# Five written orders of TensorE's four-slot blocks are replaced, and one gate comes due two slots earlier

## The chip, the cores and the metric

The kernel runs on one core of a Trainium2 chip. The time is the device time of one execution in microseconds (us). TensorE (PE) multiplies matrices into the eight banks of PSUM; ScalarE (ACT), VectorE (DVE) and GpSimd (POOL) work on the results; SyncE (SP) issues all transfers. TensorE's 128 rows are used in two ways here: as one array of 128 rows, or as two halves of 64 rows, rows 0 to 63 (half 0) and rows 64 to 127 (half 1), each with matmuls of its own.

## The reference

```python
xn = _layernorm(x, axis=-1)                       # x: 1 x 2048 x 512
qkv = (xn @ wqkv)                                 # 32 heads of 16
scores = einsum("bhqd,bhkd->bhqk", q, k) * 16**-0.5
o = einsum("bhqk,bhkd->bhqd", softmax(scores), v)
s = o.reshape(B, S, D) @ wo
h = relu(xn @ w1 + b1) ** 2                       # 512 -> 1792
g = silu(h @ w2 + b2)                             # 1792 -> 512
out = x + s * g
```

Attention with 32 heads over 2048 tokens and a dense block with a squared ReLU both start from the normalized x; their product is added to x.

## The kernel before

**Staging.** A lead-in normalizes x, makes q, k and v and parks them in DRAM. Then a loop of 512 slots does attention. A slot is one unit `u` (four heads and 512 queries; 32 units) and one block `kb` of 128 keys (16 per unit). For each slot TensorE computes four score tiles of 128 keys by 512 queries (`exp_mm`, line 1245), one per head; ACT takes exp of each into a tile `pt` in SBUF (line 1251); and two slots later four matmuls of 128 rows, one per head, add V times these to the unit's bank `po` (`pv_mm`, line 389, called by `pv_step`). In the trace each of the four appears twice, so that a po group of eight belongs to one slot, and one of sixteen to two.

**Row maxima.** The shift of the softmax needs each query's maximum over all keys before its unit starts. For a later unit, `max_mm` (line 308) computes scores with queries as rows, 128 by 512, and DVE reduces each tile to its row maxima (line 316). Fourteen or sixteen such tiles are made in four slots while they last.

**Dense work.** Between them run the matmuls of the dense block and, near the end, of the output projection (line 244 and line 806), which `dense()` yields as blocks of work for four slots. A dense matrix product is cut by rows: half 0 does its share of the sum first, half 1 adds its share to the same bank afterwards. The first product (`first_pair`) uses matmuls of 256 columns, two to a unit of work; the second (`second`) and the output projection use one of 512 columns. Dense work has one bank, `pd_t` (bufs=1): the copy out of it on ACT (line 598 or 784) must end before the next tile may start. For the same reason the first matmul that half 1 does in a bank waits (`add_manual_dep`) for a consumer of a later matmul of half 0.

**Banks of the scores.** Two rings of three banks, `se` and `pm_t`. An exp's scores go to `se` and a maximum's to `pm_t`, unless the order says otherwise. Each ring is used in turn: a matmul that takes a bank waits until the reader of the matmul three places back in that ring is done.

**The written orders.** `long_slots` issues TensorE's work of four slots from strings. Two characters are one step: a letter and the row half. `D` is a unit of dense work, `s` the scores of an exp in an `se` bank and `S` in a `pm_t` bank, `m` a maximum in a `pm_t` bank and `M` in an `se` bank. The order of TensorE is manual, so a string is the order in its queue; ACT's exps, DVE's reductions and the copies follow in the same order on their own engines, which are manual too in the loop (`LOOP`). An order is a tuple of strings, the texts; after each text comes the po group of the one or two slots that it covers (`sizes`). `pick` chooses the order of a block:

- `TWO_TWO` (two texts), `ONE_TWO_ONE` and `TWO_ONE_ONE` (three) for dense blocks while 16 or 17 exp tiles are to be had;
- `FIRST_FEW` and `SECOND_FEW` (sizes 2, 1, 1) where there are fewer than 17, which is 14: `FIRST_FEW` in the blocks at slots 4, 8 and 12, before the tiles `mt` are added at slot 16, and `SECOND_FEW` at slots 444 and 448, after the tiles `ex` have been given up;
- `MIXED` (four texts of one slot) for the block in which two tiles of the second dense product meet: six matmuls of each half end tile 0, and six of each half begin tile 1. It comes once in each of the eight chunks, at slots 44, 100, 156, 212, 268, 324, 380 and 436;
- `WO_INNER` (sizes 1, 2, 1) at slots 452, 456, 460, 468, 472 and 476 and `WO_END` (2, 1, 1) at slot 464, for the output projection of the last tokens, in which half 0 has twelve dense matmuls and half 1 has nine. From slot 480 on other orders are used again.

**The gate.** After a tile of the second dense product, `tile_post` (line 596) copies it out on ACT (`u`, line 598) and adds b2 on POOL (line 599). `gate` (line 574) then does a tanh on ACT (line 578), two steps on POOL (lines 579 and 580) and, four slots on, a store to `g_d`. `later(n, fn)` runs a step at the beginning of the n-th slot after the current one, when `begin` calls `run_waiting`, that is ahead of that slot's own work on every engine. In the chunks before the last one the gate goes through `behind` to the next po group; in the last chunk it is issued when it is due.

Of the kernel before, what the change touches and what calls it, by code (L numbers as in the profile page):

```python
# [28 lines left out]
NCK = S // CW  # L29
# [19 lines left out]
    "M0S1S0S1M1M0",  # L49
)  # L50
FIRST_FEW = (
    "D0D0S1D0M1D0S1M1D0S1D0D0m1s1D0m1D0M1D0M1S1D0D0M0S1",
    "M0s1D1D1s0m0S0D1m0D1D1D1s0D1M0D1s0S0D1D1S0D1m0D1M0",
    "s0s1m0m1S0M1",
)
SECOND_FEW = (
    "D0s1m1D0D0D0D0s1D0M1S1D0S1D0M1s1D0D0m1m1D0D0M1m1s0",
    "S1M0M0D1D1S0S0D1D1M0D1D1s0D1m0S0D1D1D1D1s0S0M0D1M0",
    "m1s0M0m0S1s1",
)  # L60
MIXED = (
    "m1s1D0m1D0m1D0s1D0M1D0D0S0s1",
    "D1D1M0S0D1D1D1s0m0S0M0D1M1S0",
    "m1D0s1D0s1D0D0m1D0s1D0S1m0M1",
    "D1D1D1M0S0D1M0D1S0S0D1M0M0S1",
)
WO_INNER = (
    "s0m1D0D0M1D0D0S1D0D0m1D0s1D0S1D0D0M1D0S1s1S1m0D0M1S0M1",
    "S0D1m0D1s0D1m0s0D1D1D1D1S0M0D1D1m0s0M1m0",
    "m0s1s0S1m1M0",  # L70
)
WO_END = (
    "M1S0M0S1D0D0m1D0D0s1S1D0D0D0D0D0M1S1D0M1s1S1D0D0m1m1M0",
    "M1S0s0m0D1D1D1m0D1s0D1m0D1s0D1s0D1m0s0D1",
    "S1M0s1m1s0m0",
)
LEAD_AT = (
    (3, 8, 12, 17, 22, 26, 31, 36, 40, 45, 48),
# [5 lines left out]
def kernel(  # L84
# [54 lines left out]
    with ExitStack() as ph:  # L139
# [87 lines left out]
        def later(n, fn, first=False):  # L227
            waiting.insert(0 if first else len(waiting), (now[0] + n, fn))
# [7 lines left out]
        def block(parts, kind, between={}):  # L236

            units, ends, posts = [[], []], [[], []], []
            for mms, per, first, post in parts:

                def emit(ms, lane, follow):
                    r = slice(64 * lane, 64 * lane + 64)
                    for out_, lh, rh, first_, last_ in ms:
                        mm = nc.tensor.matmul(  # L244
                            out_(), lh(r), rh(r),
                            start=first_ and lane == 0, stop=last_ and lane == 1,
                            skip_group_check=True,
                        )
                        if follow is not None:
                            tc.add_manual_dep(  # L250
                                mm.ins, follow.ins.name,
                                mybir.DependencyInfo(
                                    mybir.DependencyClass.Sync, mybir.DependencyReason.DATA
                                ),
                                reason="the other row tile is done with the bank",
                            )
                            follow = None

                for lane in range(2):
                    free = first and lane == 0  # L260
                    for k in range(0, len(mms), per):
                        units[lane].append(
                            lambda m=mms[k : k + per], lane=lane, k=k, free=free, emit=emit: [
                                emit(m, lane, None if k or free else last_use[0]),
                                lane and k // per in between and between[k // per](),
                            ]
                        )
                    ends[lane].append(len(units[lane]))
                posts.append(post)
            return units, ends, posts, kind  # L270

        def terms3(ps, terms):

            n = len(terms)
            out_ = []
            for t, (lh, rh) in enumerate(terms):
                for i, (a, b) in enumerate(((0, 0), (0, 1), (1, 0))):
                    out_.append((
                        ps if callable(ps) else lambda: ps,
                        lambda r, lh=lh, a=a: lh(a, r),  # L280
                        lambda r, rh=rh, b=b: rh(b, r),
                        t == 0 and i == 0, t == n - 1 and i == 2,
                    ))
            return out_
# [165 lines left out]
        def mlp_tasks(mp):  # L450
# [120 lines left out]
            def second(c):  # L571
                hT = state["hT"]

                def gate(u, tt):
                    th = rs[tt].rearrange("p a b -> p (a b)")

                    def gate_ops():
                        nc.scalar.activation(th, u, AF.Tanh, scale=0.5)
                        nc.gpsimd.tensor_scalar(th, th, 0.5, 0.5, op0=ALU.mult, op1=ALU.add)
                        nc.gpsimd.tensor_tensor(u, u, th, op=ALU.mult)  # L580
                        t0 = c * CW + tt * P
                        later(4, lambda: nc.sync.dma_start(g_d[t0 : t0 + P, :], u))

                    if c < NCK - 1:
                        behind.append(gate_ops)
                    else:
                        gate_ops()

                sums = {}

                def tile_sum(tt):
                    if tt not in sums:
                        sums[tt] = pd.tile([P, D], F32, name="pd_t")
                    return sums[tt]

                def tile_post(tt):
                    u = up.tile([P, D], F32, name="u")
                    nc.scalar.activation(u, sums[tt], AF.Copy)  # L598
                    nc.gpsimd.tensor_tensor(u, u, b2_t, op=ALU.add)  # L599
                    later(3, lambda: gate(u, tt))  # L600

                mms = []
                for tt in range(2):
                    ts_ = slice(tt * P, (tt + 1) * P)
                    mms.append(terms3(lambda tt=tt: tile_sum(tt), [
                        (
                            lambda a, q, fo=fo, ts_=ts_: hT[q, a, fo, ts_],
                            lambda b, q, fo=fo: w2t[q, b, fo],
                        )
                        for fo in range(FO)  # L610
                    ]))
                for k in range(0, 36, 12):
                    yield block([(mms[0][k : k + 12], 1, k == 0, None)], "second")
                yield block(
                    [
                        (mms[0][36:], 1, False, lambda: tile_post(0)),
                        (mms[1][:6], 1, True, None),
                    ], "mixed",
                )
                for k in range(6, 42, 12):  # L620
                    if c == NCK - 1 and k == 18:
                        gone_pt.extend(rot["ex"])
                        free_pt[:] = [t for t in free_pt if all(t is not x for x in gone_pt)]
                        tiles[0] -= 3
                    yield block(
                        [(mms[1][k : k + 12], 1, False, None if k < 30 else lambda: tile_post(1))],
                        "second",
                    )
# [532 lines left out]
        for i in range(NT + 3):  # L1161
# [32 lines left out]
            if i >= 5:  # L1194
                rest.append(("v", (i - 3) % 4, (i - 3) // 4))
                if i % 4 == 2:
                    c = (i - 3) // 4
# [409 lines left out]
```

## Time and profile before

| | us |
|---|---|
| time, median of 3 runs | 1610.49 |
| lowest and highest | 1609.7, 1610.57 |
| the profiled execution | 1609.88 |
| its span, first to last instruction | 1608.1 |
| PE busy in it | 1592.1 |
| DVE busy | 1341.7 |
| ACT busy | 1185.4 |
| granted TensorE clock | 0.999 |

The profile shows one execution. In its timeline a row has start, duration, engine, line, operation, the names of output and inputs, the number of instructions merged, and in brackets the idle time before it and what ended that. A tile's name tells the kind of matmul: `se` and `pm_t` at line 1245 are scores for an exp, at line 308 scores for a maximum, `pd_t` is dense work, `po` the product with V. The row half is not shown; it follows from the string. The ends of matmuls are modelled, their starts are recorded.

### The profile page before, as it was taken

The page shows a single profiled execution, that of the slowest core. Times are in us where ns is not written, and L with a number is a line of the kernel's source. Part 1 is how long each engine was busy: PE and PEld are TensorE (multiplying, and loading weights), DVE is VectorE, ACT ScalarE, POOL GpSimd, SP SyncE. Part 2 cuts the span into 40 slices and gives each one's busy share as a digit, 9 for nine tenths or more (in the row PEclk, how much of TensorE's full clock was granted, in tenths as well). Part 3 has the DMA queues.
Part 4 walks back from the last instruction along what each step waited for, and adds up shares of the span by engine and source line. Part 5 has one row for each costly group of instructions (what it writes and reads, how often), then busy time and mean ns, then how long its engine had stood idle before and what let it go on. Part 6 is the DMA issues. An engine that isn't in the chain of part 4 may idle for free.

```text
span 1608.1 us, 35737 instructions
## 1 busy us (share of the span) xinstructions
PE 1592.1 (99%) x13639; PEld 992.3 (62%) x13639; DVE 1341.7 (83%) x2327; ACT 1185.4 (74%) x2345; POOL 525.4 (33%) x549
## 2 busy tenths in 40 slices
PE   8999999999999999999999999999999999999998
PEld 6888666566556655665566556655665565555555
DVE  6499888988888888888888898889888998888833
ACT  6311687778778877887788778877877787777785
POOL 6645687132213310331133112302321223213334
PEclk9999999999999999999999999999999999999999
DMA  8795664334233532442243514342432432325353
GB/s 302 237 275 193 215 197 140 108 107 128 58 87 103 153 92 63 122 127 67 80 127 104 123 44 145 102 108 57 138 99 77 106 123 57 103 76 147 112 170 138
DMA packets 150467, 201.45 MB, mean 125 GB/s; under 512 B 50008, under 2 KB 67416, under 8 KB 148760
## 3 DMA queue, kind: packets, MB, share of 16 engines
q1 hardware_dynamic: 150296, 199.17, 42.2%
q8 instruction: 107, 1.75, 0.5%
q14 instruction: 64, 0.52, 0.1%
HBM read 144.84 MB, written 53.99 MB: 124 GB/s over the span
## 4 chain that ended last, share of the span: by engine, by line
PE 98%; DVE 1%; ACT 0%; issue 0%; DMA 0%; POOL 0%; DVEq 0%; SPq 0%; ACTq 0%
PE po L389 30%; PE pd_t L244 23%; PE pm_t L308 12%; PE se L1245 10%; PE se L308 6%; PE pm_t L1245 4%; PE se L1006 3%; PE se L1047 3%; PE pd_t L806 2%; PE po L1047 2%; PE pd_t L1047 1%; DVE mx L316 1%; PE pm_t L1106 1%; ACT pt L1251 0%; PE pm_t L842 0%
## 5 line engine op out<-in xcount | busy, mean ns | idle before, releaser
L316 DVE TENSOR_REDUCE mx<-pm_t 128x1 f32<-128x512 f32 x1374 | 878.6, 682 | 133.0 <-PE pm_t L308 78.8
L1251 ACT ACTIVATE pt<-se 128x512 f32<-128x512 f32 x1073 | 599.2, 620 | 82.4 <-PE pm_t L308 41.1
L308 PE MATMUL pm_t<-ka,qm 64*128 64x512 f32 x1374 | 541.2, 412 | 1.9 <-ACT pt L1251 0.7
L389 PE MATMUL po<-pt,v 128*32 128x512 f32 x3456 | 511.5, 601 | 0.0
L1245 PE MATMUL se<-qe,ka 64*128 64x512 f32 x1292 | 501.4, 421 | 0.2
L316 DVE TENSOR_REDUCE mx<-se 128x1 f32<-128x512 f32 x674 | 440.7, 682 | 57.7 <-PE se L308 29.3
L1251 ACT ACTIVATE pt<-pm_t 128x512 f32<-128x512 f32 x655 | 382.7, 609 | 136.3 <-PE pm_t L1245 86.6
L244 PEld LDWEIGHTS pd_t<-xc,w1s 64*128 64x128 f32 x2688 | 335.9, 187 | 23.0 <-ACT pt L1251 13.4
L244 PE MATMUL pd_t<-xc,w1s 64*128 64x256 f32 x2688 | 343.1, 281 | 0.0
L244 PE MATMUL pd_t<-w2t,hT 64*128 64x512 f32 x1344 | 340.9, 397 | 0.0
L308 PEld LDWEIGHTS pm_t<-ka,qm 64*128 64x128 f32 x1374 | 250.3, 184 | 96.1 <-DVE mx L316 42.0
L1245 PE MATMUL pm_t<-qe,ka 64*128 64x512 f32 x756 | 301.2, 431 | 0.0
L244 PEld LDWEIGHTS pd_t<-w2t,hT 64*128 64x128 f32 x1344 | 239.5, 184 | 78.1 <-ACT pt L1251 23.5
L1245 PEld LDWEIGHTS se<-qe,ka 64*128 64x128 f32 x1292 | 220.7, 184 | 84.0 <-ACT pt L1251 42.9
L308 PE MATMUL se<-ka,qm 64*128 64x512 f32 x674 | 254.2, 415 | 0.9
L389 PE MATMUL po<-ex,v 128*32 128x512 f32 x544 | 224.5, 601 | 0.0
L389 PEld LDWEIGHTS po<-pt,v 128*32 128x32 f32 x3456 | 95.4, 108 | 162.0 <-issue 155.8
L542 POOL TENSOR_TENSOR r<-r 128x512 f32<-128x512 f32 x56 | 58.2, 1040 | 326.2 <-ACT r L539 326.2
L308 PEld LDWEIGHTS se<-ka,qm 64*128 64x128 f32 x674 | 116.5, 184 | 76.2 <-ACT pt L1251 47.5
L1245 PEld LDWEIGHTS pm_t<-qe,ka 64*128 64x128 f32 x756 | 131.5, 184 | 18.1 <-DVE mx L316 8.4
L599 POOL TENSOR_TENSOR u<-u,b_t 128x512 f32<-128x512 f32 x16 | 20.6, 1286 | 326.4 <-ACT u L598 326.4
L1251 ACT ACTIVATE ex<-se 128x512 f32<-128x512 f32 x187 | 114.2, 624 | 10.9 <-PE pm_t L308 8.2
(139 smaller groups left out, 1410.6 us busy)
## 6 DMA issues: line engine op xcount, KB each, us to landing
w1s<-w_d SPq DMA_DIRECT2D x196, 256.0 KB
xn_d<-xT SPq DMA_DIRECT2D x8, 1024.0 KB
qm<-q_d SPq DMA_DIRECT2D x128, 64.0 KB
qe<-q_d SPq DMA_DIRECT2D x128, 64.0 KB
ka<-k_d SPq DMA_DIRECT2D x32, 256.0 KB
hl<-r_d SPq DMA_DIRECT2D x31, 256.0 KB
k_d<-hl SPq DMA_DIRECT2D x30, 256.0 KB
q_d<-hl SPq DMA_DIRECT2D x15, 512.0 KB
```

Source lines behind the costliest of these rows:

```text
L244: mm = nc.tensor.matmul(out_(), lh(r), rh(r), start=first_ and lane == 0, stop=last_ and lane == 1, skip_group_check=True,)
L308: nc.tensor.matmul(ps, qms[u][p][64 * j : 64 * j + 64, qb * P : (qb + 1) * P], kas[qd, p][64 * j : 64 * j + 64, kc * 512 : (kc + 1) * 512] ...
L316: return nc.vector.tensor_reduce(mxs[u][:, c, kc : kc + 1], ps, axis=AX.X, op=ALU.max)
L389: nc.tensor.matmul(po[32 * j : 32 * j + 32, :], vs[qd][:, (4 * kb + j) * VW : (4 * kb + j) * VW + 32], pts[j], start=(kb == 0), stop=(kb = ...
L542: nc.gpsimd.tensor_tensor(r, r, r, op=ALU.mult)
L599: nc.gpsimd.tensor_tensor(u, u, b2_t, op=ALU.add)
L806: inst = nc.tensor.matmul(ps[lane], oc[r, a, n, ts_], wot[r, b, n], start=m == 0 and (lane == 0 or wide), stop=m == kos and (lane == 1 or ...
L1006: nc.tensor.matmul(out_(), lh(slice(0, P)), rh(slice(0, P)), start=first_, stop=last_)
L1047: inst = nc.tensor.matmul(out_(), lh(r), rh(r), start=first_ and lane == lane0, stop=last_ and lane != lane0, skip_group_check=True,)
L1106: nc.tensor.transpose(pt[:, ko, :], xn[:, ko * P : (ko + 1) * P], ident)
L1245: nc.tensor.matmul(se, kas[qd, j // 2][b : b + 64, kb * P : (kb + 1) * P], qes[u][j // 2][b : b + 64, :], start=True, stop=True,)
L1251: return nc.scalar.activation(pts[j], se, AF.Exp, scale=0.25)
```

## The change

Five of the eight orders are written anew: `FIRST_FEW`, `SECOND_FEW`, `MIXED`, `WO_INNER` and `WO_END`. The number of each kind of work in a block is the same; the sequence, and with it for some matmuls the ring (small or capital letter) and the half that does a score in a given text, are others. `SECOND_FEW` has two of half 1's dense units in its third text now, which were in the second. The sizes, and `pick`, are as they were. The gate of the second tile of the last chunk becomes due one slot after its `tile_post` instead of three. As that `tile_post` now runs at slot 451 instead of 450, the gate is issued at slot 452 instead of 453.

```diff
 FIRST_FEW = (
-    "D0D0S1D0M1D0S1M1D0S1D0D0m1s1D0m1D0M1D0M1S1D0D0M0S1",
-    "M0s1D1D1s0m0S0D1m0D1D1D1s0D1M0D1s0S0D1D1S0D1m0D1M0",
-    "s0s1m0m1S0M1",
+    "D0S1M1D0D0S1m1D0D0s1D0M1S1D0D0D0M1S1D0M1S1D0D0M1m0",
+    "m0s1D1s0m0D1D1S0D1D1M0D1s0D1S0D1M0D1S0D1S0D1M0D1M0",
+    "m1s0M1S0M0S1",
 )
 SECOND_FEW = (
-    "D0s1m1D0D0D0D0s1D0M1S1D0S1D0M1s1D0D0m1m1D0D0M1m1s0",
-    "S1M0M0D1D1S0S0D1D1M0D1D1s0D1m0S0D1D1D1D1s0S0M0D1M0",
-    "m1s0M0m0S1s1",
+    "S1D0m1D0s1D0M1D0s1D0D0D0m1S1D0D0M1D0D0S1s1D0M1m1m0",
+    "m0s1D1s0D1D1m0s0D1D1m0D1s0m0D1D1D1s0s0S0D1m0M1",
+    "D1s0D1M0S1S0M0m1",
 )
 MIXED = (
-    "m1s1D0m1D0m1D0s1D0M1D0D0S0s1",
-    "D1D1M0S0D1D1D1s0m0S0M0D1M1S0",
-    "m1D0s1D0s1D0D0m1D0s1D0S1m0M1",
-    "D1D1D1M0S0D1M0D1S0S0D1M0M0S1",
+    "M1D0S1D0s1m1s1D0D0S1D0D0m0M1",
+    "m0D1D1s0D1D1m0s0D1m0D1s0s1m0",
+    "D0M1D0S1D0M1s1m1D0D0S1D0m1s0",
+    "M0D1s0m0D1S0D1s0D1S0D1D1M1M0",
 )
 WO_INNER = (
-    "s0m1D0D0M1D0D0S1D0D0m1D0s1D0S1D0D0M1D0S1s1S1m0D0M1S0M1",
-    "S0D1m0D1s0D1m0s0D1D1D1D1S0M0D1D1m0s0M1m0",
-    "m0s1s0S1m1M0",
+    "M0S1D0D0S1D0M1s1S1D0D0m1D0D0s1D0m1D0D0D0s1m1D0M1S0s1m0",
+    "s0D1M0S0D1D1m0S0M0D1D1D1s0D1m0D1D1s0m0m1",
+    "S0M1M1S1m0s0",
 )
 WO_END = (
-    "M1S0M0S1D0D0m1D0D0s1S1D0D0D0D0D0M1S1D0M1s1S1D0D0m1m1M0",
-    "M1S0s0m0D1D1D1m0D1s0D1m0D1s0D1s0D1m0s0D1",
-    "S1M0s1m1s0m0",
+    "S1M0D0S1M0D0D0M1S1D0D0s1D0m1D0S1D0s1D0D0D0m1M1D0M1m1S0",
+    "D1s0D1m0D1S0D1m0D1s0D1D1s0M0D1S0S0D1m0M1",
+    "m0s1m0S0s1M1",
 )
...
-                    later(3, lambda: gate(u, tt))
+                    later(1 if c == NCK - 1 and tt else 3, lambda: gate(u, tt))
```

## The prediction

> **What bounds the kernel now.** I read the page first, then a table of windows, then the timelines of single engines.
>
> ```profile
> span 1608.1 us, 35737 instructions
> ...
> PE 1592.1 (99%) x13639; PEld 992.3 (62%) x13639; DVE 1341.7 (83%) x2327; ACT 1185.4 (74%) x2345; POOL 525.4 (33%) x549
> ```
>
> TensorE (PE) is never free for long, so the end is the sum of its stretches, and 99% does not say whether a stretch is full: a matmul that waits for its row half still counts. I therefore cut the loop into its blocks of four slots, from one group of po matmuls (line 389) to another. Columns: window, its length, then busy time by engine.
>
> ```profile
> 290.78:302.90 12.12, 12.03 (x90) 6.11 (x89) 10.98 (x21) 9.39 (x19) 1.30 (x1) 1.00 0.04 16
> ...
> 1362.67:1373.82 11.15, 11.15 (x90) 6.18 (x88) 9.93 (x17) 8.26 (x17) 3.71 (x4) 1.00 0.52 126
> ...
> 1384.98:1397.07 12.09, 11.98 (x91) 6.05 (x89) 10.59 (x18) 9.35 (x19) 3.15 (x3) 1.00 0.66 192
> 1408.18:1419.73 11.55, 11.46 (x91) 5.93 (x89) 10.11 (x17) 8.48 (x17) 0.00 (x0) 1.00 0.37 90
> ...
> 1431.28:1442.90 11.62, 11.49 (x87) 6.10 (x85) 10.32 (x18) 9.34 (x19) 2.93 (x4) 1.00 0.16 48
> ...
> 1466.26:1477.80 11.54, 11.46 (x87) 6.08 (x86) 9.89 (x17) 9.38 (x19) 2.71 (x4) 1.00 0.51 146
> ...
> 1501.07:1512.75 11.68, 11.49 (x88) 6.13 (x86) 10.24 (x17) 8.89 (x18) 2.56 (x3) 1.00 0.56 154
> ```
>
> From the top: the first of eight MIXED blocks (slot 44); a block with the untouched ONE_TWO_ONE (slot 428); the last MIXED (slot 436; mean of the eight 12.15); the first of two SECOND_FEW (slot 444); the first of six WO_INNER (slot 452); WO_END (slot 464); the last WO_INNER (slot 476; mean of the six 11.66). With three FIRST_FEW blocks (slots 4, 8, 12) twenty blocks change. In none of these rows are ACT or DVE busy for the whole window, so neither sets its length alone.
>
> Next, the PE of slot 456, WO_INNER, whose first text begins s0 m1 D0 D0 M1 D0 D0 S1 D0 D0 m1 (letter: kind of matmul, digit: row half).
>
> ```profile
> 1442.90 1.07 PE L389 MATMUL po<-pt,v 128*32 128x512 f32 x8
> 1443.90 0.50 PE L1245 MATMUL se<-qe,ka 64*128 64x512 f32 x1
> ...
> 1444.24 0.39 PE L308 MATMUL se<-ka,qm 64*128 64x512 f32 x1
> 1444.24 0.40 PE L806 MATMUL pd_t<-wot,oc 64*128 64x512 f32 x1
> 1444.47 0.38 PE L1245 MATMUL pm_t<-qe,ka 64*128 64x512 f32 x1
> 1444.47 0.62 PE L806 MATMUL pd_t<-wot,oc 64*128 64x512 f32 x2
> ...
> 1444.93 0.39 PE L806 MATMUL pd_t<-wot,oc 64*128 64x512 f32 x1
> ...
> 1446.52 0.39 PE L806 MATMUL pd_t<-wot,oc 64*128 64x512 f32 x1
> ...
> 1447.27 0.49 PE L308 MATMUL pm_t<-ka,qm 64*128 64x512 f32 x1 [0.18 <-ACT pt L1251]
> ...
> 1447.84 0.42 PE L1245 MATMUL pm_t<-qe,ka 64*128 64x512 f32 x1
> ...
> 1448.19 1.07 PE L389 MATMUL po<-pt,v 128*32 128x512 f32 x8
> ...
> 1451.83 1.92 PE L389 MATMUL po<-pt,v 128*32 128x512 f32 x16
> 1453.68 0.49 PE L308 MATMUL pm_t<-ka,qm 64*128 64x512 f32 x1
> ...
> 1454.25 0.39 PE L308 MATMUL se<-ka,qm 64*128 64x512 f32 x1
> ...
> 1454.57 1.06 PE L389 MATMUL po<-pt,v 128*32 128x512 f32 x8
> ```
>
> **Turns.** Each half takes a matmul of 512 columns every 0.23 us (1444.24, 1444.47), the first after a po group 0.34 (1443.90 to 1444.24). M1, fifth in the text, starts with the first D0, and S1, eighth, with the second: the halves do not start in text order; one runs ahead by up to three entries of the other. So a text of n turns (its longer half) should run 0.34+0.23(n-2) from first start to last.
>
> **Floors.** A po group of eight adds 1.20: 1.00 from its start to the next text (1442.90, 1443.90), 0.32 from the last start to it (1454.25, 1454.57), 0.11 for the long first turn, less one turn. One of sixteen (1451.83, 1453.68) adds 1.85+0.32+0.11-0.23 = 2.05. Slot 428 has 29 turns and groups of 8, 16, 8 in 11.15. So WO (28 turns, same groups) could take 10.92; SECOND_FEW (29) 11.15; MIXED (28 turns, four groups of eight, 2x1.20-2.05 = 0.35 more) 11.27. Above these floors lie 8x0.88 = 7.0 in MIXED, 6x0.74 = 4.4 in WO_INNER (mean 11.66), 0.6 in WO_END, 0.8 in SECOND_FEW: 12.8 us is all that this change can reach.
>
> **What holds the halves up.** Same text of slot 456, on ACT:
>
> ```profile
> 1445.45 0.60 ACT L1251 ACTIVATE pt<-pm_t 128x512 f32<-128x512 f32 x1 [0.42 <-PE pd_t L806]
> ...
> 1446.63 1.08 ACT L1251 ACTIVATE pt<-pm_t 128x512 f32<-128x512 f32 x2
> ```
>
> The bank of S1 was written from 1444.47 to 1444.85, yet its exp starts at 1445.45, after ACT idled 0.42 for a D matmul. In the text four D0 stand ahead of this S1; the fourth runs from 1444.93 to 1445.32. A matmul is reported done only when all before it in the program are: running ahead physically does not free its bank. The second S1 (exp at 1446.63, over at 1447.23) holds the bank that m0 needs, three pm_t tiles later; m0 starts at 1447.27 instead of 1446.75, right after the D0 of 1446.52. The text's last start (1447.84) is 3.94 after its first instead of 0.34+13x0.23 = 3.33.
>
> ```profile
> PEld pd_t L244 <- ACT pt L1251: 36.9, 44, 0.8
> ```
>
> A D needs no bank from an exp, still 44 of them waited for one, 36.9 us in all: a waiting matmul also holds what stands behind it, whichever half.
>
> **MIXED**, slot 436, fourth text (D1D1D1M0S0...), PE and DVE:
>
> ```profile
> 1394.87 0.49 PE L308 MATMUL se<-ka,qm 64*128 64x512 f32 x1
> ...
> 1395.43 0.39 PE L244 MATMUL pd_t<-w2t,hT 64*128 64x512 f32 x1
> ...
> 1396.13 1.00 PE L308 MATMUL se<-ka,qm 64*128 64x512 f32 x2
> ...
> 1395.89 1.89 DVE L316 TENSOR_REDUCE mx<-se 128x1 f32<-128x512 f32 x3 [0.63 <-PE se L308]
> ```
>
> M0 is over at 1395.36, but three D1 stand ahead of it, the third until 1395.82; DVE starts at 1395.89. The fourth M0, on the first one's bank, starts at 1396.64 (1396.13 and 1.00 less its 0.49) instead of 1396.36: 0.28 lost. In a run DVE takes one every 0.60 ((1.89-0.69)/2, its last 0.69 long), ACT one every 0.48 (1.08-0.60 at 1446.63).
>
> Third text (m1D0s1D0...):
>
> ```profile
> 1388.87 0.50 PE L308 MATMUL se<-ka,qm 64*128 64x512 f32 x1
> ...
> 1391.39 0.60 ACT L598 ACTIVATE u<-pd_t 128x512 f32<-128x512 f32 x1
> ...
> 1391.81 0.49 PE L308 MATMUL pm_t<-ka,qm 64*128 64x512 f32 x1
> 1392.05 0.49 PE L244 MATMUL pd_t<-w2t,hT 64*128 64x512 f32 x1
> ```
>
> The first D0 opens the pd_t bank that copy u must empty: 0.24 late.
>
> **The change part by part.** No matmul, exp or reduce is added or removed, only their order and, for some, the bank. I walked each new text with these steps: turns of 0.23, done in program order, ACT every 0.48, DVE every 0.60, a bank free 0.05 to 0.1 after its reader ends (1447.23 to 1447.27 above).
>
> *MIXED.* Text four, M0D1s0m0D1S0..., releases M0 at 0.4; its bank is asked for at 1.26 to 1.49, and DVE is through at 1.2: 0.28 gone. Text two now has two exps ahead of copy u in ACT's queue instead of three, and they are released at 0.7 and 1.2; u starts at about 1.8 into the text instead of 2.5 (1391.39 less 1388.87), and is over before text three begins at 2.9 (1391.81): 0.24 gone. Late next are s1, m1, s1 in text one, which stand ahead of a D0 due at 0.57. They need banks that the text before has filled last:
>
> ```profile
> 1386.80 0.60 ACT L1251 ACTIVATE pt<-se 128x512 f32<-128x512 f32 x1 [0.51 <-PE pd_t L244]
> ```
>
> ACT is through with that text half a microsecond ahead of the first exp of text one, so I leave text one as it is. 8x(0.28+0.24) = 4.2.
>
> *WO_INNER.* First text M0S1D0D0S1D0M1s1S1D0D0m1...: by the walk every bank is free within 0.05 of its turn (closest: s1 after D0D0D0, m1 after S1), so 3.33 instead of 3.94 in slot 456, and about 0.58 a block. The other texts keep what they have. Five blocks: 2.9.
>
> *Gate and slot 452.* SECOND_FEW now ends its D1 in the third text, and the gate is due at slot 452 instead of 453.
>
> ```profile
> 1430.28 0.61 ACT L598 ACTIVATE u<-pd_t 128x512 f32<-128x512 f32 x1
> ...
> 1430.97 1.28 POOL L599 TENSOR_TENSOR u<-u,b_t 128x512 f32<-128x512 f32 x1 [27.04 <-ACT u L598]
> ...
> 1437.33 0.68 ACT L578 ACTIVATE r<-u 128x512 f32<-128x512 f32 x1
> ```
>
> Now the tanh comes 5 us after POOL's sum and waits for nothing. Moved, it stands ahead of all exps of slot 452. Copy u starts about 1.0 into the third text, POOL ends 0.69+1.28 later at 3.0, the text of slot 452 begins at 2.1: ACT stands until 3.0, spends 0.68, and its first exp starts 1 us late. Behind it wait that bank's m1 and the D0 after it; the text runs to 4.1, 0.8 above 3.33, the block to 10.92+0.8+0.1 = 11.8 where it took 11.62. So slot 452 loses 0.2 rather than gaining 0.58. Bounds: from that gain (sum ready earlier) to a loss of 0.8; I take -0.2, since the durations are rows. The gate's two POOL steps and its g_d store move by the same slots; POOL had idled for 27 us, and SP gets no issue that it did not have.
>
> *WO_END*: the walk finds no bank late in text one and two late by 0.05 in text two: 0.4 of the 0.62 above its floor. *SECOND_FEW*: of the 0.40 above its floor text one gives nearly all back, but text two, now one turn shorter, ends on a bank 0.1 late and on weights that come no earlier: 0.2 each, 0.4. *FIRST_FEW*:
>
> ```profile
> 181.28 0.18 PEld L244 LDWEIGHTS pd_t<-xc,w1s 64*128 64x128 f32 x1 [0.24 <-DMA xc<-xn_d]
> ```
>
> In slot 4 a D waits for xc to land, which no order changes; in slots 8 and 12 the half that holds the D runs without a gap. Nothing; between a loss and a gain of 0.3.
>
> Sum: 4.2+2.9-0.2+0.4+0.4 = 7.7. Span 1608.1 to 1600.4; the profiled run 1609.88 to 1602.2; the median of the runs, 1610.49, is 0.6 above the profiled one: **1602.8**.
>
> A rule against it: the Trainium skill, "TensorE: Matmul & The Clock Gate", Part 3, says that matmuls are monotone in start and end by program order, with only weight loads pulled ahead. The trace agrees for the end (1445.45) and not for the start (1444.24). What it would give is the first rival.
>
> **Rivals.** *Starts in text order.* Then only pairs side by side in the text share a turn. Counted so, FIRST_FEW goes from 31 to 30 turns, SECOND_FEW 33 to 31, MIXED 33 to 33, WO_INNER 31 to 32, WO_END 32 to 31: -3-4+0+6-1 = -2 turns, -0.5 us: 1610.0, and the change does not do what it says. The page named above is this rule. Against it: the two rows at 1444.24.
>
> *All floors reached*: -12.8, 1597.7. For it: weights also come early once nothing stalls. Against: three exps in a row, ACT at 0.48.
>
> *A held half holds both*, on the slower side: in MIXED's text one, s1 m1 s1 stand ahead of D0. If ACT were four exps and a copy behind there, the last bank would come free at 4x0.48+0.61 = 2.5, D0 2 us late, 8x2 = 16 against 7.7: 1618.8. It decides from 1.4 us a block ((7.7+3.3)/8). Against: the 0.51 that ACT idles at 1386.80.
>
> **How the numbers follow.** The walk 0.77, its own range 1598 to 1607 (half to all of its terms, and the gate's bounds); text-order starts 0.11; floors 0.07; held half 0.05. The range 1597 to 1607 takes in the floors and leaves out text-order starts and the held half. 0.2% is 3.2 us, about what a measurement of this kernel can tell from no change. Faster by more: 0.81 (the walk less 0.03, and the floors); within: 0.14; slower: 0.05.
>
> **What would show it.** MIXED windows near 11.6, WO_INNER near 11.1, slot 452 near 11.8 with the tanh ahead of the exps; no ACT idle of 0.4 behind a D. Wrong if D's start late behind waiting s or m in the new texts, or if the starts follow the text.

## The result and the profile after

The changed kernel takes 1602.22 us (median of four runs, 1601.52 to 1602.5), the kernel before, run beside it, 1610.29 (1609.7 to 1610.57): a ratio of 0.995, 95% interval 0.9932 to 0.9967. The profiled execution took 1601.52 us with a span of 1599.7, 8.4 less than the 1608.1 before. The forecast was 1602.8.

The page, and the same blocks as before in the table of windows (columns: window, its length, busy time by engine), from the top FIRST_FEW (slot 4), MIXED (slot 44), the untouched ONE_TWO_ONE (slot 428), MIXED (436), SECOND_FEW (444), WO_INNER (452), WO_END (464) and WO_INNER (476):

```profile
span 1599.7 us, 35747 instructions
...
PE 1585.6 (99%) x13639; PEld 991.5 (62%) x13639; DVE 1343.2 (84%) x2327; ACT 1183.2 (74%) x2345; POOL 525.2 (33%) x549
```

```profile
178.54:190.73 12.19, 12.04 (x115) 7.49 (x113) 9.96 (x17) 8.64 (x18) 8.38 (x13) 1.00 0.94 319
290.79:302.38 11.59, 11.59 (x90) 5.74 (x89) 10.96 (x21) 9.16 (x19) 1.29 (x1) 1.00 0.09 33
1358.70:1369.85 11.15, 11.15 (x90) 6.18 (x88) 9.93 (x17) 8.26 (x17) 3.50 (x4) 1.00 0.56 134
1381.03:1392.60 11.57, 11.57 (x90) 6.11 (x89) 10.69 (x18) 9.17 (x19) 3.15 (x3) 1.00 0.68 193
1403.74:1415.07 11.33, 11.33 (x90) 6.42 (x88) 9.99 (x17) 8.54 (x18) 0.00 (x0) 1.00 0.36 92
1426.47:1438.29 11.82, 11.48 (x88) 5.85 (x86) 10.25 (x18) 9.42 (x20) 5.23 (x5) 1.00 0.47 147
1460.30:1471.43 11.13, 11.13 (x87) 6.37 (x85) 10.05 (x17) 9.22 (x19) 2.69 (x4) 1.00 0.46 130
1493.44:1504.44 11.00, 11.00 (x87) 5.92 (x86) 10.00 (x17) 8.79 (x18) 2.58 (x3) 1.00 0.55 147
```

PE's share of the span says 99% in both profiles: the page cannot show this gain, the windows can. Cut at the po groups, all 127 blocks of the loop compare like this:

| blocks | before, sum | after, sum | difference |
|---|---|---|---|
| 8 MIXED | 97.17 | 92.73 | -4.44 |
| 6 WO_INNER | 69.94 | 66.84 | -3.10 |
| of these slot 452 | 11.63 | 11.82 | +0.19 |
| 1 WO_END | 11.54 | 11.14 | -0.40 |
| 2 SECOND_FEW | 23.09 | 22.72 | -0.37 |
| 3 FIRST_FEW | 34.81 | 34.85 | +0.04 |
| 107 others | | | +0.03 |

The gain stands where it was made, and the blocks between neither add to it nor give it back. Now the first text of slot 456 on PE (rows: start, duration, engine, line, tiles, count, idle time before and what ended it), with M0 S1 D0 D0 S1 D0 M1 at its head:

```profile
1439.28 0.49 PE L308 MATMUL se<-ka,qm 64*128 64x512 f32 x1
...
1439.62 0.39 PE L806 MATMUL pd_t<-wot,oc 64*128 64x512 f32 x1
1439.62 0.39 PE L1245 MATMUL pm_t<-qe,ka 64*128 64x512 f32 x1
1439.85 0.39 PE L806 MATMUL pd_t<-wot,oc 64*128 64x512 f32 x1
1439.85 0.39 PE L308 MATMUL se<-ka,qm 64*128 64x512 f32 x1
...
1442.61 0.39 PE L308 MATMUL pm_t<-ka,qm 64*128 64x512 f32 x1
1442.94 0.64 PE L389 MATMUL po<-pt,v 128*32 128x512 f32 x4
```

and on ACT:

```profile
1439.85 1.09 ACT L1251 ACTIVATE pt<-pm_t 128x512 f32<-128x512 f32 x2 [0.29 <-PE pm_t L1245]
1440.82 0.60 ACT L1251 ACTIVATE pt<-se 128x512 f32<-128x512 f32 x1
1441.30 0.62 ACT L1251 ACTIVATE pt<-pm_t 128x512 f32<-128x512 f32 x1
```

Fifteen turns take 3.33 from first to last start, where they took 3.94, and ACT no longer idles behind a D: the exp of the S1 that starts at 1439.62 follows at 0.48 from the one before it.

MIXED, slot 436. In the second and third text copy u is early, and D0 opens the third text without a wait (PE's first pair, at 1387.85):

```profile
1386.81 0.59 ACT L598 ACTIVATE u<-pd_t 128x512 f32<-128x512 f32 x1
...
1387.85 0.50 PE L244 MATMUL pd_t<-w2t,hT 64*128 64x512 f32 x1
1387.85 0.50 PE L308 MATMUL se<-ka,qm 64*128 64x512 f32 x1
```

In the fourth, DVE takes the first M0 0.54 after its start, where it took 1.02 (1395.89 less 1394.87 before), so that the last M0 starts 1.54 after the first one and not 1.77:

```profile
1390.72 0.50 PE L308 MATMUL se<-ka,qm 64*128 64x512 f32 x1
...
1391.26 0.69 DVE L316 TENSOR_REDUCE mx<-se 128x1 f32<-128x512 f32 x1 [0.38 <-PE se L308]
```

And slot 452, with the tanh ahead of its exps:

```profile
1427.07 1.28 POOL L599 TENSOR_TENSOR u<-u,b_t 128x512 f32<-128x512 f32 x1 [27.55 <-ACT u L598]
...
1428.38 0.63 ACT L578 ACTIVATE r<-u 128x512 f32<-128x512 f32 x1 [0.41 <-POOL u L599]
...
1428.72 0.39 PE L806 MATMUL pd_t<-wot,oc 64*128 64x512 f32 x1
...
1428.92 1.07 ACT L1251 ACTIVATE pt<-pm_t 128x512 f32<-128x512 f32 x2
...
1429.55 0.49 PE L308 MATMUL pm_t<-ka,qm 64*128 64x512 f32 x1 [0.34 <-ACT pt L1251]
1429.55 0.49 PE L806 MATMUL pd_t<-wot,oc 64*128 64x512 f32 x1
```

The tanh waits for POOL's sum, the first exp of the slot starts 1.46 after the text (1427.46), and m1, on the bank of that exp's scores, waits until 1429.55. The D0 behind it needs nothing of that exp. It was due one turn after the D0 of 1428.72, at 1428.95, yet it starts with m1: a matmul that waits for its bank holds the other half too.

### The profile page after: what moved, and what is told of

Read it like the earlier page. It is cut to its first block, busy times and chain, and to the rows that moved or that the text cites. A ratio compares the mean times of both kernels' runs of the same rounds, so it can differ in the third digit from the quotient of the medians.

```text
span 1599.7 us, 35747 instructions
## 1 busy us (share of the span) xinstructions
PE 1585.6 (99%) x13639; PEld 991.5 (62%) x13639; DVE 1343.2 (84%) x2327; ACT 1183.2 (74%) x2345; POOL 525.2 (33%) x549
## 4 chain that ended last, share of the span: by engine, by line
PE 98%; DMA 1%; SPq 0%; ACT 0%; DVE 0%; issue 0%; POOL 0%; DVEq 0%; ACTq 0%
PE po L389 30%; PE pd_t L244 22%; PE pm_t L308 12%; PE se L1245 11%; PE se L308 6%; PE pm_t L1245 5%; PE se L1006 3%; PE se L1047 3%; PE pd_t L806 2%; PE po L1047 1%; PE pd_t L1047 1%; PE pm_t L1106 0%; DMA xc<-xn_d 0%; DMA xt<-in_A_x_dram 0%; PE pm_t L842 0%; PE se L890 0%
## 5 line engine op out<-in xcount | busy, mean ns | idle before, releaser
L316 DVE TENSOR_REDUCE mx<-pm_t 128x1 f32<-128x512 f32 x1389 | 889.3, 684 | 129.0 <-PE pm_t L308 75.3
L1251 ACT ACTIVATE pt<-se 128x512 f32<-128x512 f32 x1101 | 616.8, 620 | 86.7 <-PE pm_t L308 47.2
L308 PE MATMUL pm_t<-ka,qm 64*128 64x512 f32 x1389 | 547.5, 411 | 1.2 <-DVE mx L316 0.6
L1245 PE MATMUL se<-qe,ka 64*128 64x512 f32 x1312 | 511.4, 420 | 0.0
L316 DVE TENSOR_REDUCE mx<-se 128x1 f32<-128x512 f32 x659 | 432.3, 683 | 52.1 <-PE se L308 33.9
L1251 ACT ACTIVATE pt<-pm_t 128x512 f32<-128x512 f32 x626 | 365.9, 609 | 125.2 <-PE pm_t L1245 81.3
L1245 PE MATMUL pm_t<-qe,ka 64*128 64x512 f32 x736 | 290.5, 428 | 0.0
L1245 PEld LDWEIGHTS se<-qe,ka 64*128 64x128 f32 x1312 | 225.7, 184 | 84.1 <-ACT pt L1251 43.9
L308 PE MATMUL se<-ka,qm 64*128 64x512 f32 x659 | 243.8, 414 | 0.0
L1245 PEld LDWEIGHTS pm_t<-qe,ka 64*128 64x128 f32 x736 | 127.2, 184 | 16.9 <-DVE mx L316 6.7
```

What stands on the lines that cost most here:

```text
L308: nc.tensor.matmul(ps, qms[u][p][64 * j : 64 * j + 64, qb * P : (qb + 1) * P], kas[qd, p][64 * j : 64 * j + 64, kc * 512 : (kc + 1) * 512] ...
L316: return nc.vector.tensor_reduce(mxs[u][:, c, kc : kc + 1], ps, axis=AX.X, op=ALU.max)
L1245: nc.tensor.matmul(se, kas[qd, j // 2][b : b + 64, kb * P : (kb + 1) * P], qes[u][j // 2][b : b + 64, :], start=True, stop=True,)
L1251: return nc.scalar.activation(pts[j], se, AF.Exp, scale=0.25)
```

## Experiments

The theories: **A**, as in the prediction: the halves run ahead of each other by up to three entries, a bank is handed over in the order of the text, and a matmul that waits for its bank holds both halves. **B**: starts in text order. **C**: the gain is from which ring and half a score goes to. **D**: the blocks gain only together. Windows are compared with the profile of the kernel before or of the changed one; a run given without an interval or a range was timed once.

**MIXED alone, WO alone.** The kernel before with the new MIXED only, and with the new WO_INNER and WO_END only.

> The kernel before with the new MIXED alone. Theory A (halves run ahead by a few entries, but a matmul's bank is handed over in the order of the text): the eight MIXED blocks fall from 12.15 to about 11.6, as they do with the whole change, so 4.0 to 4.8 us of time and nothing elsewhere. Theory B (starts in text order): 33 turns before and after, no change. Theory D (the blocks only gain together, because each leaves its banks to the next): less than half of 4.4.

> The kernel before with the new WO_INNER and WO_END alone, the gate as before at slot 453. Theory A: all six WO_INNER blocks near 11.0 (slot 452 too, with no tanh ahead of its exps), WO_END 11.1: 6 x 0.65 + 0.4 = 4.3 us. Theory B: one turn more in WO_INNER, 1 us slower. If the slot 452 of the changed kernel is long by its new text and not by the gate, slot 452 stays at 11.8 and the gain is 3.5.

MIXED alone: 1606.3 us (median of ten) beside 1610.79, 4.5 less; ratio 0.9985, interval 0.9962 to 1.0007. That interval takes in no change. The profiled execution is the slowest of the ten (1623.86 us, mean granted clock 0.949): its 107 blocks outside the five orders take 1187.31 together, against 1172.37 in the profile before. Yet each of its eight MIXED blocks is 0.38 to 0.52 shorter than before; the first, which was 12.12:

```profile
293.32:305.00 11.68, 11.68 (x91) 5.60 (x89) 10.97 (x21) 9.14 (x19) 1.29 (x1) 0.95 0.08 30
```

So MIXED gains by itself; how much in time, only the median says. WO alone: 1606.47, 4.3 less; ratio 0.9972, interval 0.9961 to 0.9984; its windows for slots 452, 456 and 464:

```profile
1432.15:1443.18 11.03, 11.03 (x88) 5.90 (x86) 10.16 (x18) 9.21 (x19) 2.89 (x3) 1.00 0.11 32
1443.18:1454.16 10.98, 10.98 (x88) 5.87 (x86) 10.52 (x21) 8.79 (x18) 3.53 (x3) 1.00 0.66 206
1465.14:1476.28 11.14, 11.14 (x88) 6.29 (x86) 10.06 (x17) 9.24 (x19) 2.73 (x4) 1.00 0.55 154
```

Neither gain needs the other orders, so D falls, and B's extra turn in WO_INNER is not there. Slot 452 reaches 11.03 with the new text: the 0.79 more that it takes in the changed kernel is not the text's. The two medians fall by 8.8 together, 0.7 more than the whole change. By the blocks that should be 0.4: the 0.79 of slot 452, less the 0.37 of SECOND_FEW, which is in neither run. The medians don't tell 0.4 from 0.7.

**The gate.** In the changed kernel, and alone in the kernel before:

```diff
-                    later(1 if c == NCK - 1 and tt else 3, lambda: gate(u, tt))
+                    later(2 if c == NCK - 1 and tt else 3, lambda: gate(u, tt))
```

> The changed kernel with the last gate due two slots after its tile instead of one, so at slot 453 as in the kernel before. If the tanh ahead of the exps is the price of slot 452: 11.82 falls to about 11.05, the total by 0.8 us to about 1601.4. If the new text is at fault: no change.

> The kernel before with the last gate one slot earlier, at slot 452. Its tile is copied out in the second text there, so POOL's sum is ready at the start of slot 452. If the price is the wait for that sum: slot 452 changes by less than 0.2 us, though the tanh stands ahead of all exps. If the price is the tanh's place as such (0.68 us on ACT): slot 452 is longer by 0.4 or more.

With the gate at slot 453 in the changed kernel: 1601.42 us (median of four, 1601.22 to 1602.56). That is the total that was expected, but it confirms nothing: the four times overlap those of the changed kernel (1601.52 to 1602.5), and the profiled span is 1599.7, just that of the changed kernel. Slots 452 and 464, and two of SP's waits between 1425 and 1465 (engine, line waited for: us in total, times, longest):

```profile
1426.14:1437.32 11.18, 11.18 (x88) 6.08 (x86) 10.22 (x18) 9.48 (x20) 3.32 (x4) 1.00 0.16 51
1459.31:1471.35 12.04, 11.57 (x88) 6.36 (x86) 10.15 (x17) 9.40 (x19) 3.11 (x4) 1.00 0.54 142
```

```profile
SPq L738 <- ACT r L578: 6.5, 1, 6.5
SPq L436 <- POOL hl L429: 3.5, 1, 3.5
```

Slot 452 gives back 0.64 of its 0.79, and slot 464, which the expectation left out, takes 0.90. The first load of `g` (line 738) waits for the tanh, and all that SP issues later stands behind it. In the changed kernel that wait is 2.9 and this load goes out at 1431.12; here it is 6.5 and the load goes out at 1434.44. The unit's normalization (line 427) moves from 1447.39 to 1450.97, its store (line 436) from 1450.77 to 1454.35, and the shift rows that slot 464's scores need follow the store:

```profile
1458.22 2.02 SPq L380 DMA_DIRECT2D qe<-sh_d  x4
...
1460.84 0.47 PE L1245 MATMUL pm_t<-qe,ka 64*128 64x512 f32 x1 [0.47 <-DMA qe<-sh_d]
```

These four transfers are issued from 1458.22 to 1460.24, with a po group at 1459.31 and the slot's text behind it, whose first score waits for them; in the changed kernel from 1454.78 to 1456.80, 3.5 ahead of that group. So the early gate has a use: it lets SP go. How much it is worth is less sure. WO alone has its gate at slot 453 too, and its slot 464 takes 11.14: there the transfers begin at 1463.25, 1.9 ahead of the po group at 1465.14, here 1.1 ahead. So they come 0.8 later here against that group, and the text starts 0.53 late (1460.84 instead of 1460.31): with the gate at slot 453 there had been about 0.3 to spare. From the tanh to the transfers SP's chain took 25.5 there and 26.5 here; why stays open. The 0.90 was seen in one profile.

Alone in the kernel before, one slot earlier, the gate changes slot 452 from 11.63 to 11.61, though the tanh stands ahead of the exps there. Its price is then the wait for POOL's sum and not its place; the next run shows the same in the new text.

**Both at once.** The changed kernel with the old SECOND_FEW, which copies the tile in its second text, the gate still at slot 452, and the first text of SECOND_FEW dealt alternately from its own two sequences:

```diff
-    "S1D0m1D0s1D0M1D0s1D0D0D0m1S1D0D0M1D0D0S1s1D0M1m1m0",
-    "m0s1D1s0D1D1m0s0D1D1m0D1s0m0D1D1D1s0s0S0D1m0M1",
-    "D1s0D1M0S1S0M0m1",
+    "D0s1D0m1D0s1D0M1D0S1D0S1D0M1D0s1D0m1D0m1D0M1D0m1s0",
+    "S1M0M0D1D1S0S0D1D1M0D1D1s0D1m0S0D1D1D1D1s0S0M0D1M0",
+    "m1s0M0m0S1s1",
...
-                    later(1 if c == NCK - 1 and tt else 3, lambda: gate(u, tt))
+                    later(2 if c == NCK - 1 and tt else 3, lambda: gate(u, tt))
```

> The changed kernel with the old SECOND_FEW, of which the first text is dealt alternately, and the last gate at slot 452: its tile is copied in the second text, so that POOL's sum is ready when the tanh comes, and SP's loads behind the tanh still go out early. If slot 452 paid for the wait for that sum and slot 464 (with the gate at 453) for SP's wait: slot 452 near 11.1, slot 464 at 11.15, slots 444 and 448 near 11.2, so 0.7 + 0.3 = 1.0 us less than the changed kernel, 1601.2. If slot 464 depends on something else, it stays near 12.0 and the total at 1602.

1599.82 us (median of five, 1599.39 to 1600.55), 2.4 below the changed kernel; ratio to the kernel before 0.9933, interval 0.992 to 0.9945. Slots 444, 448, 452, 464:

```profile
1403.06:1414.17 11.11, 11.11 (x90) 6.12 (x88) 9.93 (x17) 8.40 (x17) 0.00 (x0) 1.00 0.38 94
1414.17:1425.34 11.17, 11.17 (x91) 6.31 (x89) 9.95 (x17) 9.31 (x19) 0.29 (x1) 1.00 0.08 18
1425.34:1436.38 11.04, 11.04 (x87) 5.78 (x85) 10.14 (x18) 9.06 (x19) 4.92 (x5) 1.00 0.52 161
1458.37:1469.52 11.15, 11.15 (x88) 6.33 (x86) 10.06 (x17) 9.23 (x19) 2.71 (x4) 1.00 0.49 137
```

Slots 444 and 448 are at their floor of 11.15; slots 452 and 464 are 0.12 and 0.23 above theirs of 10.92. Slot 452 has the tanh ahead of its exps and takes no more than with the gate elsewhere (11.03). Together the four take 1.2 us less than in the changed kernel, where 1.0 was expected. Another 0.8 of this profile is slot 4 (11.38), which is 11.6 to 12.2 in the other profiles, whichever FIRST_FEW they have.

**Order alone.** The kernel before with each half's old sequence of letters in MIXED and WO_INNER, the two sequences dealt alternately; then the same with the last pair of MIXED's first and third text turned round. First texts:

```diff
 MIXED, text one
-    "m1s1D0m1D0m1D0s1D0M1D0D0S0s1",
+    "m1D0s1D0m1D0m1D0s1D0M1D0s1S0",   first run
+    "m1D0s1D0m1D0m1D0s1D0M1D0S0s1",   second run
 WO_INNER, text one, both runs
-    "s0m1D0D0M1D0D0S1D0D0m1D0s1D0S1D0D0M1D0S1s1S1m0D0M1S0M1",
+    "s0m1D0M1D0S1D0m1D0s1D0S1D0M1D0S1D0s1D0S1D0M1D0M1m0D0S0",
```

> The kernel before; in MIXED and WO_INNER each half keeps the old sequence of letters of every text, and only the two sequences are dealt out alternately. Theory A: text three and four of MIXED lose their 0.24 and 0.28, text one of WO_INNER about half of its 0.6 (by the walk M1 and m0 at its end still meet a bank that DVE frees late): 8 x 0.5 + 6 x 0.3 = 5.8 us in all, MIXED blocks near 11.6, WO_INNER near 11.35. Theory C (the gain is from which ring and which half a score goes to, not from the sequence of the halves): no change.

> The kernel before with both halves dealt alternately, as in the run that gained nothing in MIXED, but with the last pair of its first and third text in the other order, half 0 first. If D1 at the head of texts two and four waited for the exp or reduction that follows the last D0, and that one stood behind half 1's in its engine's queue: these texts start 0.52 behind the po group again instead of 0.77 to 0.96, and MIXED falls to 11.6. If D1 waits for something else: no change, 12.17.

The first run gained almost nothing of the 5.8 us expected: 1609.62 beside 1610.41, ratio 0.9995, interval 0.9986 to 1.0005. WO_INNER fell by 0.24 to 0.32 a block, as expected. MIXED stayed at 12.15 to 12.36, as C has it: inside the texts most of the late starts were gone (in most blocks 0.05 left in text three, 0.01 in text four), but texts two and four began 0.77 to 0.97 behind the last po start instead of 0.52. From slot 380 of that run, the exp of S0 and the weight load of D1 at the head of text two:

```profile
1232.26 0.60 ACT L1251 ACTIVATE pt<-pm_t 128x512 f32<-128x512 f32 x1
...
1232.91 0.18 PEld L244 LDWEIGHTS pd_t<-w2t,hT 64*128 64x128 f32 x1 [1.14 <-ACT pt L1251]
```

D1 may enter the bank when the consumer of half 0's first score after its last D0 is done (the manual dependency). Dealing had put half 1's s1 ahead of S0, and its exp ahead in ACT's queue. The second run turns that pair:

```profile
1226.39 0.59 ACT L1251 ACTIVATE pt<-pm_t 128x512 f32<-128x512 f32 x1
...
1227.21 0.18 PEld L244 LDWEIGHTS pd_t<-w2t,hT 64*128 64x128 f32 x1 [0.84 <-ACT pt L1251]
```

1604.32 us beside 1610.78, ratio 0.996, interval 0.9945 to 0.9975. The exp is over at 1226.98, 0.23 before D1 could start anyway, and the eight MIXED blocks are 11.42 to 11.76 (sum 92.22, below the 92.73 of the new order). For MIXED C falls: the old letters, in a better order, gain as much. For WO_INNER it doesn't: the old letters give 0.28 of the 0.66 a block, and the rest came only with the new letters, which choose other rings and halves. The expectation had laid that rest to a bank that DVE frees late; no run parts that from C.

**One lopsided text.** The changed kernel, fourth text of MIXED; each half's sequence is kept:

```diff
-    "M0D1s0m0D1S0D1s0D1S0D1D1M1M0",
+    "D1D1D1M0s0m0D1S0D1s0S0D1M1M0",
```

> The changed kernel; in the fourth text of MIXED the first three D1 are pulled ahead of everything, as in the old text, while each half keeps its new sequence and every score its ring. Theory A: M0 is handed over only behind the third D1, DVE ends it at 1.7 instead of 1.2, and M1 on its bank starts at 1.75 instead of 1.5: the text loses 0.25 to 0.3, 2.2 us over eight blocks, with DVE idle behind a D. Theory C: no change. Theory B: the three D1 run alone, two turns or 0.46 a block.

MIXED is longer by 0.30 to 0.41 in each block (0.38 on average), the run 1604.89. Slot 380, whose text begins at 1235.46, first on PE, then on DVE:

```profile
1235.46 0.50 PE L244 MATMUL pd_t<-w2t,hT 64*128 64x512 f32 x1
1235.47 0.49 PE L308 MATMUL se<-ka,qm 64*128 64x512 f32 x1
...
1236.50 0.69 DVE L316 TENSOR_REDUCE mx<-se 128x1 f32<-128x512 f32 x1 [0.92 <-PE pm_t L308]
```

DVE idles, and takes M0 1.03 after its start instead of 0.53; the last pair starts at 1.78 instead of 1.5. That is 0.25; the other 0.1 is the last pair, whose weights now come no earlier than the matmuls. The three D1 do not run alone: M0 starts beside the first of them. A holds here; B and C do not.

**How far ahead.** The changed kernel, first text of WO_INNER:

```diff
-    "M0S1D0D0S1D0M1s1S1D0D0m1D0D0s1D0m1D0D0D0s1m1D0M1S0s1m0",
+    "M0S1D0D0D0D0D0D0D0D0S1M1s1S1D0m1D0s1D0m1D0s1S0m1M1m0s1",
```

> The changed kernel; in the first text of WO_INNER eight D0 stand in a row ahead of the second S1, each half's sequence unchanged. It measures how far a half can run ahead: with no limit S1 starts at 0.34 into the text; with three entries, as read from the old texts, S1 starts with the fifth D0, near 1.3. Theory B: with the eighth, near 2.0. The text gets longer by 1 us or more in each of the six blocks under the last two.

PE in slot 456, whose text begins at 1439.56:

```profile
1439.89 1.32 PE L806 MATMUL pd_t<-wot,oc 64*128 64x512 f32 x5
1440.83 0.49 PE L1245 MATMUL pm_t<-qe,ka 64*128 64x512 f32 x1
```

Five D0 start at 0.23 from each other, the fifth at 1440.82, and S1 starts with it, while the last three of the eight still wait. Three entries, then. The block took 12.33 instead of 11.02; slot 452, long already, took 12.32 instead of 11.82.

**Copy u.** The changed kernel with `...m0D1s0s1m0` turned to `...m0s0D1s1m0` at the end of MIXED's second text.

> The changed kernel; in the second text of MIXED the last D1 and the s0 ahead of it trade places, so that three exps instead of two stand ahead of copy u in ACT's queue, as before the change. If the number of exps ahead made the old copy late: text three loses its 0.24 again, 1.9 us in all. If the late release of the old exps did: the copy starts 0.5 later, still over when text three begins, and no more than 0.05 a block is lost.

MIXED is longer by 0.02 to 0.13 a block (0.08 on average), run 1602.04. So the third exp made up about 0.08 of the 0.24, a little more than the 0.05 expected. That the rest was the late release of the old exps is what is left over; no run shows it by itself.

## Why the prediction was right

**The floors** from the rows of slot 428 held: WO_INNER runs at 10.99 to 11.02 (slot 452 apart) for a floor of 10.92, and SECOND_FEW in the version with the sum ready at 11.11 and 11.17 for 11.15.

**MIXED**, forecast 4.2, measured 4.44. From first to last start text three, of which 0.24 was forecast, shrank by 0.22 to 0.24 in seven of eight blocks, and text four, of which 0.28 was forecast, by 0.23 to 0.28 in all. In slot 212 text three had been 0.43 late and is still 0.24 late. Text one did stay: it lost its 0.13 in four blocks and got it in the other four.

**WO_INNER**, forecast 2.9 for five blocks, measured 3.29: 0.66 a block instead of 0.58. The starts of text one give 0.61 of it; the po groups, too, follow the last start a little sooner. **Slot 452**, forecast to lose 0.2 and to take 11.8: +0.19, 11.82, by the steps given. **WO_END**, 0.4: 0.40. **SECOND_FEW**, 0.4: 0.37. **FIRST_FEW**, nothing: +0.04, which is luck. Slots 8 and 12, said to run without a gap, gained 0.13 each. Slot 4 took 0.30 more, between POOL's split of thl and the landing of xc (0.49 and 0.27 of idle weight loads), but at the full clock it varies by that much between profiles of one order (11.62 to 11.94 with the old one, 11.38 to 12.19 with the new).

**One row was misread.** The 44 waits of a D for an exp, 36.9 us, do not show a held half. Each is 0.84, and in the trace before the first weight load of each text of slot 436 has 0.84 of idle time ahead of it, whatever it loads. Two of the four:

```profile
1385.97 0.18 PEld L308 LDWEIGHTS pm_t<-ka,qm 64*128 64x128 f32 x1 [0.84 <-ACT pt L1251]
...
1388.86 0.18 PEld L244 LDWEIGHTS pd_t<-w2t,hT 64*128 64x128 f32 x1 [0.84 <-ACT pt L1251]
```

These are texts that begin on time, 1.00 behind the po group: the 0.84 is the time of that group, counted for whatever ended last before it. No term of the sum rests on the 36.9. That a waiting matmul holds both halves is right all the same; slot 452 of the changed kernel shows it.

**What the prediction did not see** is the other side of the gate. It said that SP gets no issue that it did not have, and counted the gate's own store only; it left out that SP's first load waits for the tanh. In the one profile with the gate left at slot 453, slot 464 lost 0.90 and slot 452 gained 0.64. The forecast of the total did not depend on it, since the gate was moved.

**The rivals.** Starts in text order: the run with eight D0 ahead excludes it, and so does MIXED alone, which gained with as many turns by that count. A held half: the mechanism is there (slot 452 is one), but not at MIXED's first text. All floors reached: 12.8 was the bound; the changed kernel took 8.1, the version with the sum ready 11.0, of which 0.8 is slot 4's own spread.

## What to carry to other kernels

When two row halves share TensorE, write their order so that each consumer's matmul has nothing of the other half ahead of it that ends later: three entries of lead cost nothing in turns, but the bank is handed over only in program order, and a late bank stops both halves. Mind also a wait that the program itself adds, such as D1's here for the score behind the last D0. Read such stalls by cutting the trace at a repeated group and setting each text's starts against turns; the share of busy time does not show them. Before a step is moved for one engine's sake, see which queue (here SP's) stands behind it, and whether its input is ready at the new place.

## What the runs showed of the hardware

- Starts of matmuls on two row halves are not in program order: a half runs up to three entries ahead, and the fourth waits (S1 with the fifth of eight D0). The Trainium skill, "TensorE: Matmul & The Clock Gate", Part 3, has them monotone in start; this trace does not agree.
- The reports to other engines do come in program order: an M0 that started beside the first of three D1 that stand ahead of it was taken by DVE 1.03 after its start, 0.53 without them ahead (slot 380).
- A matmul that waits for its bank holds the other half as well: a D0 due at 1428.95 started at 1429.55, with the m1 ahead of it that waited for an exp.
- ACT takes an exp of 0.60 to 0.62 every 0.48 and DVE a reduction of 0.68 every 0.60 when neither waits.
